# Spreading W_down's sums over the gate/up pairs, placing GpSimd's part beside PSUM reads, moving two pairs' weight prefetches into pass 0's last down product, and putting four additions first there

## The chip, the cores and the metric

The kernel runs on one core of a Trainium2 chip. The metric is the time of one execution in microseconds (us), measured on the device. Engines are named as in the profile: PE is TensorE's matmul, PEld its weight load, DVE VectorE, ACT ScalarE, POOL GpSimd, SP SyncE; "SPq" marks SyncE's queue, which here only issues DMAs. TensorE writes its results into banks of PSUM; to evacuate a bank is to read the result out, after which TensorE may use the bank again. SBUF holds everything else.

## The reference

A pre-norm linear-attention block with a residual, then a pre-norm gated MLP with a residual, all in bf16. The sequence has 2048 tokens, the model width is D = 1024, and the MLP is F = 3584 wide. The change touches the MLP only:

```python
def _B_ref(x, W_gate, W_up, W_down):
    gate = jnp.einsum("bsd,df->bsf", x, W_gate)
    up = jnp.einsum("bsd,df->bsf", x, W_up)
    gate = gate * (gate > 0)                       # shortened
    h = gate * up
    return jnp.einsum("bsf,fd->bsd", h, W_down)

h = x + _A_ref(_layernorm(x), A_wqkv, A_wo)        # attention, not touched
h2 = h + _B_ref(_layernorm(h), B_W_gate, B_W_up, B_W_down)
```

## The kernel before

Every large product is done in Strassen's manner: fewer matmuls, paid for with sums of blocks before them and after them. The MLP runs in two passes of 1024 tokens. A pass has a **gate/up stage** of 14 pairs (pair 0 to 13; a pair is two F-tiles of gate and two of up), and then a **down stage** of seven products, numbered 0 to 6. Products 0, 2 and 4 are plain; 1, 3, 5 and 6 are split once more, each into seven smaller products M1 to M7 ("level 2").

The split products need sums of blocks of W_down. They are made once, during pass 0's gate/up stage, written to DRAM (`t_scr`, `l_scr`), and loaded again chunk by chunk in the down stages, through a ring of seven buffers in SBUF (the "W_down ring"). Three kinds of sums are made: four per pair on VectorE (`WT`), four per two pairs on VectorE (`WL`, sums of the first sums), and four per two pairs on GpSimd (`WM`, from the raw weights).

```python
def wd_sums(q):                       # WT: 4 subtractions of 128x512 on VectorE, then a store
    add(0, wb(0, 1), wb(0, 0), ...)
    add(2, wb(1, 1), wb(0, 1), ...)
    add(1, wb(1, 1), wsum[:, k, 0, :], ...)
    add(3, wb(1, 0), wsum[:, k, 1, :], ...)
    dma(sl_ws[k], t_v[:, :, q, :], wsum[:, k, :, :], ...)

def wl_sums(m):                       # WL: half(0), half(1) on VectorE; WM: raw() on GpSimd
    ...
    def addw(j, x, y):
        PL.add("pool", lambda e: e.tensor_tensor(out=lsw[:, z, j, :], in0=x[0], in1=y[0], op=ALU.subtract),
               reads=x[1] + y[1], writes=[B_lsw[z][j]], name="WM%d_%d" % (j, m))
    def raw():
        addw(0, wr(0, 1), wr(0, 0)); addw(2, wr(1, 1), wr(0, 1))
        addw(1, wr(1, 1), t_(0));    addw(3, wr(1, 0), t_(1))
        dma(sl_lw[z], l_v[:, no, :, m, :], lsw[:, z], ...)
    return [lambda: half(0), lambda: half(1), raw]
```

A pair is seven products, each for gate and for up, each of eight matmuls of 512 columns. The work of the other engines is woven in through the lists `mid`. `PL` keeps one list per engine; an engine does its list strictly in order and waits by semaphores for what it reads.

```python
def strassen_pair(ps_, q, fill, mid):
    ...                                # P1 (copies of the banks on ScalarE), P5, P6
    for f_ in mid[0]: f_()             # <- place A: W_down's sums, before the evacuations of P2
    for w in range(2):
        prod(w, BA[w], w_blk(w, 1, 0), a_blk(1, 0), False, "P2")
        ...
    mul(hh[:, f1, 0:SBW], bank(BA[1]), r11[:, rr, :], ...)
    for w in range(2):
        prod(w, BB[w], t_blk(w, 2), s_blk(2), False, "P7")
        add_s5(c22[:, w, :], bank(BB[w]), B_bank[BB[w]], w, B_c22[w], "c22")   # VectorE reads PSUM
    ...
    for w in range(2):
        prod(w, BC_[w], w_blk(w, 1, 1), s_blk(3), False, "P3")
        add_s5(c12[:, w, :], bank(BC_[w]), B_bank[BC_[w]], w, B_c12[w], "c12")
    for f_ in mid[1]: f_()             # <- place B: behind P3's evacuations
    for w in range(2):
        prod(w, BB[w], t_blk(w, 3), a_blk(1, 1), False, "P4")   # its bank is free after c22
    ...
    load_w_next(); load_w_next()       # gate and up weights, two pairs ahead
```

Pair 13 was left free of sums, so that W_down's first chunks could be loaded there; pair 12 made the sums of both:

```python
wt_at = {q: [q] for q in range(NPAIR - 1)}
wt_at[NPAIR - 2].append(NPAIR - 1)           # pair 12 makes the WT sums of 12 and of 13
...
for x in wt_at.get(q, []):
    mid[0] += wl_q; wl_q.clear()
    mid[1 if q == 0 else 0].append(lambda x=x: wd_sums(x))
    if x % 2 == 1:                            # both pairs of an m are there
        w0_, w1_, wr_ = wl_sums(x // 2)
        mid[1].append(w0_); wl_q.append(w1_); mid[0].append(wr_)
        for z in (x + 1, x + 2):
            if z < NPAIR: mid[0].append(lambda z=z: load_wraw(z))   # raw W_down for the next two
if q not in wt_at:                            # pair 13
    mid[0] += wl_q + [load_wd_next] * NWS     # seven W_down loads
```

In the down stage, the results are put together from PSUM and from SBUF, some by VectorE and some by GpSimd:

```python
level2(5, YB, q_hh(1, hh), sg_x0, ev_out(1, 0, STB, B_V, out2, ...))   # needs V, the residual added
level2(6, XB, q_d4, sg_x1, ev_out(0, 1, 0, B_U, outst, ...))
at(3, 4, lambda: ld_h(0, 1))                  # residual loads
at(4, 0, lambda: ld_h(1, 1), *[add_h(U_, B_U, 0, 1, j) ...])
at(4, 2, lambda: ld_h(1, 0))
at(5, 0, *[add_h(V_, B_V, 1, 0, j) ...],      # GpSimd: V += residual, four additions
         *[p_22(j) ...],                      # GpSimd: four outputs
         e_u5(0), e_u5(1))                    # VectorE: U += PSUM ("dU5"), frees a bank
at(5, 1, e_u5(2), e_u5(3))
```

## Time and profile before

| | before |
|---|---|
| median of 3 runs, us | 735.58 (735.56 to 735.62) |
| profiled span, us | 736.1 |
| TensorE busy, us | 725.6 |
| VectorE busy, us | 561.1 |
| gate/up stage, pass 0 / pass 1, us | 170.37 / 169.21 |
| down stage, pass 0, us | 80.74 |
| last down stage to the end, us | 82.99 |

The stage lengths are differences of the start of a stage's first matmul and of the next stage's, read from the timeline.

Two lines of the profile page of before, the span and the busy time of each engine with its number of instructions:

```profile
span 736.1 us, 11563 instructions
...
PE 725.6 (99%) x4311; PEld 364.0 (49%) x4311; DVE 561.1 (76%) x976; ACT 352.3 (48%) x614; POOL 105.5 (14%) x169
```

TensorE is busy 99% of the span, so a change that keeps every matmul can win only TensorE's idle time. The list of TensorE's waits in before (engine, what it made, what it waited for; us in total, times, longest) says how much that is:

```profile
PE ps L710 <- DVE RAB L1423: 1.0, 2, 0.8
PE ps L710 <- DVE RE L1341: 0.9, 1, 0.9
...
PE ps L710 <- DMA RW<-in_B_W_down_dram: 0.5, 1, 0.5
```

The lines left out lie in the attention part. These three sum to 2.4 us in four places; the first has two. (A wait is counted from the modelled end of the matmul before it, which the records put 0.38 us after its start for 512 columns, while the starts lie 0.22 us apart. So a listed wait costs TensorE about 0.16 us more than it says, as an estimate from these records.) The place of the 0.9 us is pair 12 of pass 0. From the timeline of before there (start, length, engine, line, what it made from what, count, and in brackets the idle time before it):

```profile
377.89 1.89 PE L710 MATMUL ps<-RH,RWG 128*128 128x512 bf16 x8
...
379.49 0.77 DVE L1304 TENSOR_TENSOR RAB<-RAB 128x512 f16<-128x512 bf16 x1
...
380.90 1.04 DVE L1289 TENSOR_TENSOR RO<-RWG,RO 128x1024 f16<-128x1024 bf16 x1
381.35 2.19 POOL L694 TENSOR_TENSOR RAB<-RW,RAB 128x256 f16<-128x256 bf16 x2
381.86 1.15 DVE L1289 TENSOR_TENSOR RO<-RWG 128x1024 f16<-128x1024 bf16 x1
382.94 1.61 DVE L677 TENSOR_TENSOR RX<-RW,RX 128x768 f16<-128x768 f16 x2
384.47 3.01 DVE L655 TENSOR_TENSOR RW<-RW 128x512 f16<-128x512 bf16 x8
387.40 0.69 DVE L1345 TENSOR_TENSOR RAB<-ps,RAB 128x512 bf16<-128x512 f32 x1
388.60 1.88 DVE L1341 TENSOR_TENSOR RE<-ps,RE 128x512 bf16<-128x512 f32 x3
389.34 1.90 PE L710 MATMUL ps<-RH,RO 128*128 128x512 bf16 x8 [0.93 <-DVE RE L1341]
```

The pair starts at 377.89. VectorE makes all eight `WT` sums (L655, 384.47 to 387.40) before it reads P2's and P7's results out of PSUM (L1345, L1341); P4, at 389.34, needs a bank that the first L1341 frees, and waits 0.93 us. VectorE's sums of the next pair's weights (L1289) take 1.04 and 1.15 us beside GpSimd's sums (POOL L694), and 0.68 us elsewhere.

The other waits lie in the last two down products. From the timeline of before there:

```profile
464.79 4.50 POOL L1423 TENSOR_TENSOR RE<-RE,RX 128x512 f32<-128x512 f32 x4 [5.13 <-DVE RE L1423]
...
467.09 2.61 DVE L1423 TENSOR_TENSOR RE<-ps,RE 128x512 f32<-128x512 f32 x4 [1.77 <-POOL RE L1423]
...
469.62 2.00 DVE L1423 TENSOR_TENSOR RAB<-ps,RE 128x512 bf16<-128x512 f32 x3
470.95 1.70 PE L710 MATMUL ps<-RW,RAB 128*128 128x256 f16 x14 [0.80 <-DVE RAB L1423]
...
473.19 1.05 PE L710 MATMUL ps<-RW,RAB 128*128 128x256 bf16 x8 [0.53 <-DMA RW<-in_B_W_down_dram]
```

GpSimd adds the residual to V in four additions, 464.79 to 469.29. VectorE's four sums at 467.09 are two that read V and then two of dU5. TensorE waits 0.80 us for an output's bank and, one product later, 0.53 us for a load of W_down.

### The profile page before, as it was taken

To read this page: it belongs to the slowest core of one execution; us is meant where nothing else is said; L and a number is where in the kernel's file an instruction comes from. 1 tells how busy PE (TensorE), PEld (TensorE's weight loads), DVE (VectorE), ACT (ScalarE), POOL (GpSimd) and SP (SyncE) were. 2 spreads that over 40 slices of the span, in tenths; PEclk is the share of its full clock that TensorE was granted. 3 is DMA by queue.
4 is the path that set the end of the run, shared out by engine and by line. 5 is a ranking of instruction groups with operands and counts; after the bars stand their busy time and mean duration, and the time that the engine had idled before them with its cause. 6 is when DMAs were issued, how large, how long until landed. Compare 5 with 4: busy or idle time off the path is not lost.

```text
span 736.1 us, 11563 instructions
## 1 busy us (share of the span) xinstructions
PE 725.6 (99%) x4311; PEld 364.0 (49%) x4311; DVE 561.1 (76%) x976; ACT 352.3 (48%) x614; POOL 105.5 (14%) x169
## 2 busy tenths in 40 slices
PE   8999999999999999999999999999999999999998
PEld 3444444344444444444444666754444444447766
DVE  6887867799776999898997769865757575667594
ACT  3877756864842456777754100135454544521000
POOL 1311100000360112132220003400000000000052
PEclk9999999999999999999999999999999999999999
DMA  9633144013998889888969999983323242337892
GB/s 304 210 79 94 29 116 163 22 29 67 200 233 254 246 253 274 240 241 256 307 193 301 324 247 341 308 260 85 100 72 106 65 115 59 100 91 245 241 317 87
DMA packets 191880, 133.93 MB, mean 182 GB/s; under 512 B 51664, under 2 KB 173776, under 8 KB 191824
## 3 DMA queue, kind: packets, MB, share of 16 engines
q1 hardware_dynamic: 191152, 132.54, 63.3%
q8 instruction: 34, 0.56, 0.3%
q10 hardware_dynamic: 672, 0.66, 0.3%
q14 instruction: 22, 0.18, 0.1%
HBM read 96.47 MB, written 25.17 MB: 165 GB/s over the span
## 4 chain that ended last, share of the span: by engine, by line
PE 85%; DVE 8%; ACT 2%; DMA 2%; SPq 1%; issue 1%; POOL 0%; DVEq 0%; POOLq 0%; ACTq 0%
PE ps L710 84%; DVE RAB L1423 2%; DMA RW<-in_B_W_down_dram 1%; DVE RAB L796 1%; SPq L545 1%; ACT RX L789 1%; DVE RE L1171 1%; DMA RE<-in_A_x_dram 1%; DVE RX L793 1%; SPq L541 1%; DVE RO L1289 0%; ACT ps L715 0%; ACT RXH L748 0%; DVE RX L1012 0%; DVE RE L1423 0%
## 5 line engine op out<-in xcount | busy, mean ns | idle before, releaser
L715 ACT ACTIVATE ps<-ps 128x512 f32<-128x512 f32 x172 | 100.2, 582 | 212.6 <-PE ps L710 170.3
L710 PE MATMUL ps<-RC,RO 128*128 128x512 f16 x672 | 154.2, 379 | 0.0
L710 PE MATMUL ps<-RH,RWG 128*128 128x512 bf16 x448 | 105.9, 379 | 0.0
L710 PEld LDWEIGHTS ps<-RC,RO 128*128 128x128 f16 x672 | 65.7, 98 | 79.3
L1345 DVE TENSOR_TENSOR RAB<-ps,RAB 128x512 bf16<-128x512 f32 x56 | 38.6, 689 | 71.9 <-PE ps L710 71.9
L710 PE MATMUL ps<-RC,RWG 128*128 128x512 f16 x320 | 76.8, 380 | 0.1
L1341 DVE TENSOR_TENSOR RE<-ps,RE 128x512 bf16<-128x512 f32 x112 | 74.2, 685 | 1.6 <-PE ps L710 0.7
L710 PEld LDWEIGHTS ps<-RH,RWG 128*128 128x128 bf16 x448 | 43.8, 98 | 52.7
L710 PE MATMUL ps<-RW,RAB 128*128 128x256 f16 (+3 forms) x414 | 66.9, 318 | 1.3 <-DVE RAB L1423 0.8
L1423 POOL TENSOR_TENSOR RE<-RE,RX 128x512 f32<-128x512 f32 x16 | 23.6, 1505 | 307.1 <-DMA RX<-h_scr 298.5
L715 ACT ACTIVATE RE<-RE 128x512 bf16<-128x512 bf16 x56 | 35.1, 627 | 64.2 <-DVE RE L1341 63.6
L710 PE MATMUL ps<-RH,RO 128*128 128x512 bf16 (+1 forms) x256 | 61.3, 380 | 0.9 <-DVE RE L1341 0.9
L710 PE MATMUL ps<-RAB 128*128 128x512 bf16 (+2 forms) x274 | 59.3, 357 | 0.1
L710 PE MATMUL ps<-RW,RE 128*128 128x512 bf16 x256 | 57.6, 380 | 0.8 <-DVE RXH L1195 0.7
L715 ACT ACTIVATE RE<-ps 128x512 f32<-128x512 f32 x64 | 37.6, 597 | 35.4 <-PE ps L710 35.0
L710 PEld LDWEIGHTS ps<-RW,RAB 128*128 128x128 bf16 (+1 forms) x414 | 40.3, 98 | 25.8 <-DVE RAB L1423 1.1
L710 PEld LDWEIGHTS ps<-RC,RWG 128*128 128x128 bf16 (+1 forms) x320 | 30.0, 98 | 39.9 <-ACT ps L715 5.9
L1289 DVE TENSOR_TENSOR RO<-RWG 128x1024 f16<-128x1024 bf16 x54 | 39.7, 736 | 4.7 <-DMA RWG<-in_B_W_up_dram 4.7
L1423 DVE TENSOR_TENSOR RE<-ps,RE 128x512 f32<-128x512 f32 x40 | 27.0, 687 | 19.0 <-PE ps L710 15.8
L715 ACT ACTIVATE RAB<-ps 128x512 bf16<-128x512 f32 x56 | 33.4, 596 | 15.0 <-PE ps L710 13.9
L710 PEld LDWEIGHTS ps<-RH,RO 128*128 128x128 f16 (+1 forms) x256 | 24.2, 98 | 31.4 <-DVE RE L1341 1.8
L710 PEld LDWEIGHTS ps<-RAB 128*128 128x128 bf16 (+1 forms) x274 | 26.8, 99 | 25.4 <-issue 1.6
(138 smaller groups left out, 998.0 us busy)
## 6 DMA issues: line engine op xcount, KB each, us to landing
RWG<-in_B_W_gate_dram SPq DMA_DIRECT2D x28, 512.0 KB, 4.8
RWG<-in_B_W_up_dram SPq DMA_DIRECT2D x28, 512.0 KB, 5.9
RW<-in_B_W_down_dram SPq DMA_DIRECT2D x14, 512.0 KB, 6.0
t_scr<-RW SPq DMA_DIRECT2D x14, 512.0 KB, 3.5
RE<-in_A_x_dram SPq DMA_DIRECT2D x23, 256.0 KB, 3.4
RW<-l_scr SPq DMA_DIRECT2D x13, 448.0 KB, 6.3
l_scr<-RX SPq DMA_DIRECT2D x7, 768.0 KB, 4.5
RW<-in_B_W_down_dram SPq DMA_DIRECT2D x12, 384.0 KB, 5.3
```

The costliest lines, as they stand in the source:

```text
L541: return PL.add(eng, lambda e: e.dma_start(dst_ap, src_ap), reads=reads, writes=writes, slot=slot, name=name)
L545: return PL.add("sp", lambda e: e.dma_start_transpose(dst_ap, src_ap), reads=reads, writes=writes, slot=slot, name=name)
L710: lambda e: e.matmul(out_ap, lhsT, rhs, start=start, stop=stop, skip_group_check=skip),
L715: PL.add("act", lambda e: e.activation(out=dst, in_=src, func=func), reads=reads, writes=writes, name=name)
L789: PL.add("act", lambda e: e.activation(out=Et[:, k, :], in_=src, func=ACTF.Exp), reads=[src_buf], writes=[B_E[k]], name=name + "_exp")
L793: PL.add("dve", lambda e: e.tensor_scalar(out=Et[:, k, :], in0=Et[:, k, :], scalar1=1.0, scalar2=1e-6, op0=ALU.min, op1=ALU.add), reads=[] ...
L796: PL.add("dve", lambda e: e.scalar_tensor_tensor(out=dst_ap, in0=src, scalar=C1, in1=Et[:, k, :], op0=ALU.add, op1=ALU.max), reads=[src_bu ...
L1171: PL.add("dve", lambda e: e.tensor_tensor(out=osb[:, k, :].rearrange("p (g h e) -> p g h e", h=HPG, e=Dh), in0=nv[:, :, :, 0:Dh], in1=rden ...
L1289: PL.add(eng, lambda e: e.tensor_tensor(out=tb(j, u), in0=f0(u), in1=f1(u), op=ALU.subtract), reads=[B_w[i + x] for x in r] + ([B_T[k + x] ...
L1341: PL.add("dve", lambda e: e.tensor_tensor(out=dst, in0=src, in1=ftmp[:, w, :], op=ALU.add), reads=[bsrc, B_s5[w]], writes=[bdst], name=name)
L1345: PL.add("dve", lambda e: e.tensor_tensor(out=dst, in0=a_, in1=b_, op=ALU.mult), reads=reads, writes=[wr], name=name)
L1423: PL.add(eng, lambda e: e.tensor_tensor(out=dst, in0=in0, in1=in1, op=op), reads=reads, writes=writes, name=name)
```

## The change

The intent is to take the pile of sums out of pair 12, and to keep GpSimd from slowing VectorE. It has four parts.

- **Spread.** Each pair makes the `WT` sums of one pair; pair 13 makes its own, and the last `WL` sums. In even pairs the `WT` sums stand behind P3 (place B) rather than ahead of P2 (place A). W_down's first loads are spread over pair 13 for that, and the ring's order is rotated, since four of its buffers lie over those of the sums.
- **GpSimd.** The `WM` sums go one by one, each started when a product ends (P7 gate, P7 up, P3 gate, P3 up). VectorE then reads PSUM. The raw W_down loads are issued behind the last of the four.
- **Prefetch.** The gate and up weights of pass 1's first pairs (four loads of 512 KB) are loaded in pass 0's last down product rather than in pairs 12 and 13.
- **dU5.** All four dU5 additions stand in front of the additions that read V.

```diff
-        RING = [list(range(NWS))]
+        RING = [[NWS - 2, NWS - 1] + list(range(NWS - 2))]
 ...                                    # wl_sums
-                       reads=x[1] + y[1], ..., name="WM%d_%d" % (j, m))
+                       deps=[PL.prog["pe"][-1]], reads=x[1] + y[1], ..., name="WM%d_%d" % (j, m))
-            def raw(): ...             # four addw and the store
+            def last():
                 addw(3, wr(1, 0), t_(1))
+                if m == NM - 1:
+                    load_wd_next()
+                    load_wd_next()
                 dma(sl_lw[z], l_v[:, no, :, m, :], lsw[:, z], ...)
+                for q in (2 * m + NWR, 2 * m + NWR + 1):
+                    if q < NPAIR:
+                        load_wraw(q)
+            raw = [lambda: addw(0, ...), lambda: addw(2, ...), lambda: addw(1, ...), last]
 ...                                    # strassen_pair
                 prod(w, BB[w], t_blk(w, 2), s_blk(2), False, "P7")
+                run(mid[4], 1)
 ...
                 prod(w, BC_[w], w_blk(w, 1, 1), s_blk(3), False, "P3")
+                run(mid[4], 1)
 ...
-            load_w_next()
-            load_w_next()
+            if ps_ > 0 or q < NPAIR - 2:
+                load_w_next()
+                load_w_next()
 ...                                    # down_pass
-               lambda: e_u5(0), lambda: e_u5(1))
-            at(5, 1, lambda: e_u5(2), lambda: e_u5(3))
+               *[lambda j=j: e_u5(j) for j in range(STB)])
 ...                                    # the loop over pairs
-        wt_at = {q: [q] for q in range(NPAIR - 1)}
-        wt_at[NPAIR - 2].append(NPAIR - 1)
 ...
+                    mid[0] += wl_q
+                    wl_q.clear()
+                    if q % 2 == 0:
+                        mid[1].append(lambda: wd_sums(q))
+                    else:
+                        w0_, w1_, mid[4] = wl_sums(q // 2)
+                        mid[0].append(lambda: wd_sums(q))
+                        if q < NPAIR - 1:
+                            mid[1].append(w0_)
+                            wl_q.append(w1_)
+                        else:
+                            mid[0] = [load_wd_next] * 2 + mid[0] + [w0_, w1_]
                 strassen_pair(p_, q, fill, mid)
+                if p_ == 0 and q == NPAIR - 1:
+                    for _ in range(NWS - 4):
+                        load_wd_next()
 ...                                    # what down_pass of pass 0 also does
+                late += [(load_w_next, (6, 0))] * 2 + [(load_w_next, (6, 3))] * 2
```

More of the change, by code (lines that the diff above doesn't have):

```diff
@@ L476, in bass_sequential_preLN__linear_attn_block__glu_gated_reglu__prompt_kernel @@
             b_.over = B_wraw + flat(B_wsum)
+        for b_ in B_wd[0:2]:
+            b_.over = list(B_wraw)
         for b_ in flat(B_lsw):
@@ L601, in bass_sequential_preLN__linear_attn_block__glu_gated_reglu__prompt_kernel @@
         X_AT = [(NPAIR - 3) * 2 + i for i in range(NWX)]
-        RING = [list(range(NWS))]
-        RING.append([(len(WLIST) + i) % NWS for i in range(NWS)] +
+        RING = [[NWS - 2, NWS - 1] + list(range(NWS - 2))]
+        RING.append([RING[0][(len(WLIST) + i) % NWS] for i in range(NWS)] +
                     [NWS + (NPAIR * 2 + x) % NWG for x in X_AT])
@@ L694, in addw, with t_ @@
                 PL.add("pool", lambda e: e.tensor_tensor(out=lsw[:, z, j, :], in0=x[0], in1=y[0], op=ALU.subtract),
-                       reads=x[1] + y[1], writes=[B_lsw[z][j]], name="WM%d_%d" % (j, m))
-            def raw():
-                def t_(j):
-                    return lsw[:, z, j, :], [B_lsw[z][j]]
-                addw(0, wr(0, 1), wr(0, 0))
-                addw(2, wr(1, 1), wr(0, 1))
-                addw(1, wr(1, 1), t_(0))
+                       deps=[PL.prog["pe"][-1]], reads=x[1] + y[1], writes=[B_lsw[z][j]], name="WM%d_%d" % (j, m))
+            def t_(j):
+                return lsw[:, z, j, :], [B_lsw[z][j]]
+            def last():
                 addw(3, wr(1, 0), t_(1))
+                if m == NM - 1:
+                    load_wd_next()
+                    load_wd_next()
                 dma(sl_lw[z], l_v[:, no, :, m, :], lsw[:, z], "st_wm_%d" % m, reads=B_lsw[z], writes=[B_wscr[m]])
+                for q in (2 * m + NWR, 2 * m + NWR + 1):
+                    if q < NPAIR:
+                        load_wraw(q)
+            raw = [lambda: addw(0, wr(0, 1), wr(0, 0)), lambda: addw(2, wr(1, 1), wr(0, 1)),
+                   lambda: addw(1, wr(1, 1), t_(0)), last]
             return [lambda: half(0), lambda: half(1), raw]
@@ L1905, in bass_sequential_preLN__linear_attn_block__glu_gated_reglu__prompt_kernel @@
                     hh_sums(q - 1)
-                mid = [[], [], [], []]
+                mid = [[], [], [], [], []]
                 if p_ == 0:
@@ L1916, in bass_sequential_preLN__linear_attn_block__glu_gated_reglu__prompt_kernel @@
                         ln_q.append(n_)
-                    for x in wt_at.get(q, []):
-                        mid[0] += wl_q
-                        wl_q.clear()
-                        mid[1 if q == 0 else 0].append(lambda x=x: wd_sums(x))
-                        if x % 2 == 1:
-                            w0_, w1_, wr_ = wl_sums(x // 2)
+                    mid[0] += wl_q
[6 more added lines that the diff above has]
+                        if q < NPAIR - 1:
                             mid[1].append(w0_)
                             wl_q.append(w1_)
-                            mid[0].append(wr_)
-                            for z in (x + 1, x + 2):
-                                if z < NPAIR:
-                                    mid[0].append(lambda z=z: load_wraw(z))
-                    if q not in wt_at:
-                        mid[0] += wl_q + [load_wd_next] * NWS
-                        wl_q.clear()
+                        else:
+                            mid[0] = [load_wd_next] * 2 + mid[0] + [w0_, w1_]
                 strassen_pair(p_, q, fill, mid)
+                if p_ == 0 and q == NPAIR - 1:
+                    for _ in range(NWS - 4):
+                        load_wd_next()
                 if p_ == 1 and q >= NPAIR - 3:
```

## The prediction

> **What bounds it now.** TensorE. The page's busy table gives 725.6 of 736.1 us; the chain of waits is 85% TensorE. In the gate/up stage (220 to 380 us) the table of windows shows 94 to 95 matmuls per 20 us; the timeline has eight 512-column matmuls in 1.73 us, 216 ns each, the warm rate of the Trainium skill ("TensorE: Matmul & The Clock Gate", "Wait — 56ns, not 53.3ns?": 215.7 ns). The change alters no matmul, only ring slots. It can win only idle TensorE time, and the list of waits has little:
> - 0.93 us at 389.3 (last-but-one pair, pass 0), released by VectorE: W_down's last two F-tile pairs are summed together there, eight 0.4 us subtractions ahead of the evacuations;
> - 0.80 us at 470.9, released by VectorE, and 0.53 us at 473.2, released by a W_down load (last down products of pass 0);
> - 0.18 us at 720.3, VectorE, the same place in pass 1.
>
> Sum 2.4 us (0.33%). The rest is untouched.
>
> **Pair 12, pass 0.** Four sums and two level-2 sums (2.7 us of VectorE) go to pair 13, which makes no sums for a next pair. The 0.93 us gap should vanish.
>
> **Last down products.** All four dU5 additions now stand before the additions that wait 1.77 us for GpSimd (at 467.1). Two of them (1.3 us) fill that idle time, so the bank is free 1.3 us earlier: the 0.80 and 0.18 us gaps go. But the next product's W_down load lands at 473.14, behind a chain of SyncE issues (454.2 to 465.0, one transpose issue of 5.1 us in it) and an 8.1 us transfer with the DMA engines full (share above 1). The change moves none of these, so the 0.80 us mostly reappears as a longer wait for this load (0.53 to about 1.3 us): 0.2 us won.
>
> **Moved prefetches.** Two pairs of gate and up loads (2 MB, about 7 us at 290 GB/s) leave 389 to 406 for the last product (475 to 487). Issued near 480, they should land near 487; VectorE wants them near 485, TensorE at 497. VectorE loses 1 to 2 us, TensorE nothing. W_down's third chunk loads only after GpSimd's last sum, some 11.3 us into pair 13, and is needed at 17.2; such a load took 5.7 us. Tight.
>
> **GpSimd.** Its 28 sums (0.67 us at best, up to 1.19) now each start after a product ends, beside VectorE's PSUM reads. The Trainium skill ("SBUF — State Buffer", "SBUF: two separate sides") says that GpSimd and a VectorE instruction with two SBUF inputs exclude each other; the trace agrees: VectorE sums of 0.68 us took up to 1.15 us. VectorE regains a few us, worth nothing.
>
> **Sum.** 735.6 − 0.93 − 0.18 − 0.2 = 734.3 us. Range 733.1 to 735.5. Chances: faster by over 2% 0.005, within 2% 0.99, slower 0.005.
>
> **Right or wrong shown by:** no wait over 0.2 us between 380 and 400; near 470 no VectorE release and a W_down release of 1 to 1.5 us; no TensorE wait in the first down product (402 to 415) or at pass 1's start (483 to 500); GpSimd's sums nearer 0.67 us; TensorE busy unchanged at 725.6.
>
> **Wrong if:** the last product's load lands earlier (733.2 or so); the late third W_down chunk or late gate/up weights stall TensorE by 1 to 3 us (736 to 738); VectorE's moved sums delay evacuations in the even pairs, seven times over.

## The result, and the profile after

| | before | after |
|---|---|---|
| median of 6 runs, us | 735.6 (734.93 to 736.43) | 734.4 (733.69 to 735.02) |
| ratio, with 95% interval | | 0.9983 (0.9970 to 0.9996) |
| gate/up stage, pass 0, us | 170.37 | 169.21 |
| down stage, pass 0, us | 80.74 | 79.87 |
| last down stage to the end, us | 82.99 | 83.67 |
| VectorE busy, us | 561.1 | 554.0 |

A ratio is the mean time of one kernel's fast runs over the mean of the other's of the same rounds, so it is not quite the ratio of the medians. The change wins about 1.2 us. The profiled spans differ by 3.0 us, and that must not be read as the gain. The profiled execution of before took 737.83 us, more than any run in the table, and 1.65 us of the difference lies at the start: the gate/up stage of pass 0 begins at 232.79 us in before and at 231.14 us in after, long before anything that was changed; between 10 and 20 us the granted TensorE clock was 0.85 in that trace and 1.00 in after's.

The same lines of the page of after:

```profile
span 733.1 us, 11513 instructions
...
PE 719.6 (98%) x4253; PEld 363.4 (50%) x4311; DVE 554.0 (76%) x976; ACT 352.7 (48%) x614; POOL 104.5 (14%) x169
```

TensorE's busy time seems to have shrunk by 6 us. It has not: 58 of the 4311 matmul records are missing from this trace (x4253), while the weight loads are all there. So busy times of TensorE are not compared; the starts of matmuls and the listed waits are. One of the missing records is pass 1's first matmul: the trace's first is at 480.44, but its weight load starts at 480.11, and in before, where both are recorded, the matmul starts 0.11 us after that load. So the down stage is taken to end at 480.22, in all traces with this gap 0.22 us before the first matmul recorded. The weight loads alone give the same gain for the stage, 0.86 us. TensorE's waits in after:

```profile
PE ps L718 <- DVE RAB L1434: 1.5, 2, 0.9
```

The list has more lines, all of them outside the MLP. L1434 is L1423 of before; the line numbers moved. Both waits are in down stages: 0.64 us in pass 0 and 0.87 us in pass 1. The wait in pair 12 and the one for W_down are gone. Pair 12 in after, at the same two products:

```profile
384.56 2.00 DVE L1349 TENSOR_TENSOR RE<-ps,RE 128x512 bf16<-128x512 f32 x3
...
386.75 1.67 PE L718 MATMUL ps<-RH,RO 128*128 128x512 bf16 x7
...
387.42 1.54 DVE L657 TENSOR_TENSOR RW<-RW 128x512 f16<-128x512 bf16 x4
```

VectorE has evacuated P7 and P3 before it makes sums, and the sums are four; they stand behind P3. P4 (386.75; one of eight records is missing) does not wait. GpSimd's sums now lie in pair 13, where this is the last of the four:

```profile
398.93 0.67 POOL L696 TENSOR_TENSOR RAB<-RW,RAB 128x256 f16<-128x256 bf16 x1 [0.19 <-PE ps L718]
398.94 0.68 DVE L1349 TENSOR_TENSOR RE<-ps,RE 128x512 bf16<-128x512 f32 x1
399.67 0.90 SPq L543 DMA_DIRECT2D RW<-in_B_W_down_dram  x2
400.35 1.89 PE L718 MATMUL ps<-RE,RAB 128*128 128x512 bf16 x8
```

The four of pair 13 take 0.67 us each, here beside VectorE's evacuation of PSUM, which takes its usual 0.68 us. In the six odd pairs before it the first of four still takes 0.92 us, so that the mean of all 28 falls only from 0.79 to 0.75 us. VectorE's mean for the sums that GpSimd used to slow fell from 736 to 684 ns. The third W_down chunk is issued at 399.67, as soon as GpSimd's last sum allows it. The down stage starts at 400.35 and never waits for that chunk.

The last two down products in after:

```profile
462.10 4.50 POOL L1434 TENSOR_TENSOR RE<-RE,RX 128x512 f32<-128x512 f32 x4 [5.26 <-DMA RX<-h_scr]
...
464.41 1.42 DVE L1434 TENSOR_TENSOR RE<-ps,RE 128x512 f32<-128x512 f32 x2 [0.71 <-POOL RE L1434]
...
466.64 2.01 DVE L1434 TENSOR_TENSOR RAB<-ps,RE 128x512 bf16<-128x512 f32 x3 [0.81 <-POOL RE L1434]
467.98 3.23 PE L718 MATMUL ps<-RE,RAB 128*128 128x256 f16 x28 [0.64 <-DVE RAB L1434]
```

The dU5 additions are out of the way. Yet VectorE's outputs start at 466.64, just as GpSimd's fourth addition ends (462.10 + 4.50 = 466.60), and TensorE waits for them as it did. In before they started at 469.62, 0.33 us after that end (469.29): this is all that the dU5 additions had held up. Counted from the start of the down stage (403.16 in before, 400.35 in after), TensorE goes on after this wait at 67.79 us in before and at 67.63 us in after. That is a gain of 0.16 us, though the residual's load landed 0.12 us later in the stage. The rest of the stage's gain of 0.87 us is the load's wait, which is not there.

The moved prefetches show on VectorE only. From the timeline of after, at pass 1's start (480.22):

```profile
484.55 0.69 DVE L1297 TENSOR_TENSOR RO<-RWG 128x1024 f16<-128x1024 bf16 x1 [3.43 <-DMA RWG<-in_B_W_up_dram]
```

VectorE waits 3.43 us for the up weights of the next pair. No wait of TensorE follows.

### The profile page after: what moved, and what is told of

It reads as the page before. It is cut to its first block, busy times and chain, and to the rows that moved or that the text cites. A ratio compares the mean times of both kernels' runs of the same rounds, so it can differ in the third digit from the quotient of the medians.

```text
span 733.1 us, 11513 instructions
## 1 busy us (share of the span) xinstructions
PE 719.6 (98%) x4253; PEld 363.4 (50%) x4311; DVE 554.0 (76%) x976; ACT 352.7 (48%) x614; POOL 104.5 (14%) x169
## 4 chain that ended last, share of the span: by engine, by line
PE 86%; DVE 5%; ACT 3%; issue 2%; DMA 2%; SPq 1%; POOL 0%; POOLq 0%; ACTq 0%; DVEq 0%
PE ps L718 86%; SPq L543 1%; DVE RAB L804 1%; DMA RE<-in_A_x_dram 1%; DVE RE L1179 1%; ACT RX L797 1%; ACT RXH L756 1%; DMA RE<-RE 1%; DVE RX L801 1%; DVE RX L1020 1%; POOL RE L1434 0%; DMA RX<-h_scr 0%; ACT ps L723 0%; DVE RW L914 0%; DVE RXH L1203 0%
## 5 line engine op out<-in xcount | busy, mean ns | idle before, releaser
L1434 POOL TENSOR_TENSOR RE<-RE,RX 128x512 f32<-128x512 f32 x16 | 23.5, 1494 | 288.2 <-DMA RX<-h_scr 288.2
L718 PE MATMUL ps<-RW,RAB 128*128 128x256 f16 (+3 forms) x399 | 62.5, 312 | 0.3
L718 PE MATMUL ps<-RH,RO 128*128 128x512 bf16 (+1 forms) x228 | 55.3, 379 | 1.5
L718 PE MATMUL ps<-RAB 128*128 128x512 bf16 (+1 forms) x254 | 53.7, 350 | 0.3
L718 PEld LDWEIGHTS ps<-RW,RAB 128*128 128x128 f16 (+1 forms) x404 | 39.6, 98 | 21.2
L1297 DVE TENSOR_TENSOR RO<-RWG 128x1024 f16<-128x1024 bf16 x54 | 36.9, 684 | 8.3 <-DMA RWG<-in_B_W_up_dram 8.3
L1434 DVE TENSOR_TENSOR RE<-ps,RE 128x512 f32<-128x512 f32 x40 | 27.0, 688 | 18.1 <-PE ps L718 15.4
L718 PEld LDWEIGHTS ps<-RW,RE 128*128 128x128 bf16 x256 | 23.9, 98 | 29.1 <-DVE RXH L1203 1.2
```

The lines of the kernel that those rows point to most:

```text
L718: lambda e: e.matmul(out_ap, lhsT, rhs, start=start, stop=stop, skip_group_check=skip),
L1297: PL.add(eng, lambda e: e.tensor_tensor(out=tb(j, u), in0=f0(u), in1=f1(u), op=ALU.subtract), reads=[B_w[i + x] for x in r] + ([B_T[k + x] ...
L1434: PL.add(eng, lambda e: e.tensor_tensor(out=dst, in0=in0, in1=in1, op=op), reads=reads, writes=writes, name=name)
```

## The experiments

Twelve runs were made, ten of edited kernels and one each of before and after again. Times are compared by their ratios. All gave correct results. The times first, each with its ratio against before in the same rounds. Then the two stages of pass 0 in the profiled run, and all of TensorE's waits there from 0.17 us on.

| kernel | median, us | ratio (95%) | gate/up | down | waits in pass 0: gate/up; down |
|---|---|---|---|---|---|
| before (first trace) | 735.6 | | 170.37 | 80.74 | 0.93 VectorE; 0.80 VectorE, 0.53 load |
| before_again | 736.4 | 1.0007 (0.9989 to 1.0024) | 171.73 | 80.53 | 0.96 VectorE and three small; 0.80 load, 0.27 VectorE |
| after | 734.4 | 0.9983 (0.9970 to 0.9996) | 169.21 | 79.87 | none; 0.64 VectorE |
| control | 733.77 | 0.9975 (0.9963 to 0.9988) | 169.22 | 79.96 | none; 0.74 VectorE |
| undo_eu5 | 733.97 | 0.9982 (0.9969 to 0.9994) | 169.22 | 80.54 | none; 0.47 load, 0.55 VectorE |
| undo_spread | 733.29 | 0.9974 (0.9961 to 0.9986) | 169.21 | 80.60 | none; 1.39 load |
| undo_prefetch | 734.74 | 0.9988 (0.9974 to 1.0002) | 169.24 | 80.92 | none; 0.45 load, 0.65 VectorE |
| only_pool | 736.6 | 1.0014 (1.0000 to 1.0029) | 171.96 | 80.74 | 1.28 and three smaller, VectorE; 0.57 load, 0.52 VectorE |
| undo_pool | 734.36 | 0.9982 (0.9969 to 0.9995) | 169.22 | 80.23 | none; 0.80 VectorE |
| undo_both | 735.09 | 0.9992 (0.9979 to 1.0004) | 170.46 | 80.82 | 1.08 VectorE; 1.37 VectorE |
| pool_place | 734.35 | 0.9988 (0.9974 to 1.0002) | 169.21 | 80.88 | none; 0.94 load, 0.54 VectorE |
| ht_early | 732.79 | 0.9971 (0.9958 to 0.9983) | 169.21 | 79.25 | none; none |
| split_adds | 736.12 | 1.0015 (1.0002 to 1.0028) | 169.21 | 80.56 | none; 1.33 VectorE |
| split_only | 735.83 | 1.0017 (1.0004 to 1.0030) | 169.21 | 80.94 | none; 1.71 VectorE |

In the nine traces in which the record of pass 1's first matmul is missing, the down stage is taken to end 0.22 us before the first one recorded, as in after. The stage that nothing disturbs, pass 1's gate/up, then took 169.2 us in all fourteen traces (169.11 us in each by the weight loads, which are all there). So stages compare far more finely than the times of whole runs do.

### control

The changed kernel as it is.

> The changed kernel again, unedited, to see which differences of the two traces come back. Between the two traces on hand the stages differ so: pair 12 of pass 0 takes 12.1 us against 13.2, the down stage of pass 0 79.9 against 80.7, the last down stage to the end 83.7 against 83.0, everything before pair 12 differs by 1.7 us (clock warm-up and start, not the change). Theory S (the differences are systematic): the same lengths within 0.2 us, the VectorE wait of 0.9 us near the end of pass 1's down stage again, time 734.4, ratio to before 0.998. Rival N (pass 1's 0.9 us wait and the early W_down load are chance): the wait in pass 1 is back near 0.2 us, or the W_down wait near 470 us is back.

733.77 us (732.89 to 733.98), ratio 0.9975: the gain is there again. The 0.74 us wait for VectorE in the last down products is there again too, and no wait for W_down. Pass 1 shows no wait at all in its down stage, where after's trace had 0.87 us. The same code therefore gives 0 and 0.87 us at that place, and nothing there is put down to the change.

### undo_eu5

The dU5 part taken back.

```diff
-               *[lambda j=j: e_u5(j) for j in range(STB)])
+               lambda: e_u5(0), lambda: e_u5(1))
+            at(5, 1, lambda: e_u5(2), lambda: e_u5(3))
```

> The changed kernel with the four dU5 additions at their old places (two after the second down sub-product). As predicted blind: VectorE is 1.3 us later at the bank, so the wait near 468 us grows from 0.64 to about 1.9 us less slack, and the time by 0.5 to 1.3 us in pass 0 and as much in pass 1. Rival (after reading the trace: the two outputs wait for GpSimd's fourth addition, which waits for the residual load, and the dU5 additions stand in idle time either way): the wait grows by at most 0.3 us in each pass, time at most 0.6 us longer.

The wait for VectorE is 0.55 us, not longer than the 0.64 and 0.74 us of the changed kernel, but a load's wait of 0.47 us ahead of it hides part of it. The time, 733.97 us, is within noise of control's. What the time can't resolve, the timeline of undo_eu5 shows:

```profile
461.89 4.50 POOL L1434 TENSOR_TENSOR RE<-RE,RX 128x512 f32<-128x512 f32 x4 [4.40 <-DMA RX<-h_scr]
...
466.71 2.00 DVE L1434 TENSOR_TENSOR RAB<-ps,RE 128x512 bf16<-128x512 f32 x3
```

GpSimd ends at 466.39, and the outputs start 0.33 us later, as in before. So it is in all five traces with the old place of the dU5 additions; in the seven with the new place and four additions on GpSimd, the outputs start 0.03 us after GpSimd's end. The dU5 part is worth 0.30 us in front of the outputs, of the 1.3 us that the prediction gave it; the rest was idle time either way.

### undo_spread

The pile put back: pair 12 makes the `WT` sums of both pairs ahead of P2, with the `WL` halves placed as before. GpSimd's sums stay one by one in pair 13.

```diff
-                    if q % 2 == 0:
+                    if q == NPAIR - 2:
+                        w0_, w1_, wm_ = wl_sums(q // 2)
+                        mid[0] += [lambda: wd_sums(q), lambda: wd_sums(q + 1)]
+                        mid[1].append(w0_)
+                    elif q == NPAIR - 1:
+                        mid[4] = wm_
+                        mid[0] += [load_wd_next] * 2 + [w1_]
+                    elif q % 2 == 0:
```

> The changed kernel with the sums of W_down's last F-tile pair moved back into pair 12, beside that pair's own. Theory: the 0.9 to 1.1 us TensorE wait for VectorE in pair 12 comes back whole, pair 12 is 13.1 to 13.2 us long, time up by 0.9 to 1.1 us against the control. Rival (the new places of the other sums, or GpSimd keeping off VectorE's sums, removed the wait): pair 12 stays below 12.4 us.

If the pile alone made the wait, it had to come back. It did not: pair 12 has no wait and the stage takes 169.21 us. The timeline of undo_spread in pair 12:

```profile
375.90 1.89 PE L718 MATMUL ps<-RH,RWG 128*128 128x512 bf16 x8
...
377.75 0.43 DVE L1312 TENSOR_TENSOR RAB<-RAB 128x512 f16<-128x512 bf16 x1
...
379.43 0.68 DVE L1297 TENSOR_TENSOR RO<-RWG 128x1024 f16<-128x1024 bf16 x1
380.03 1.14 DVE L679 TENSOR_TENSOR RX<-RW,RX 128x768 f16<-128x768 f16 x2
381.09 3.02 DVE L657 TENSOR_TENSOR RW<-RW 128x512 f16<-128x512 bf16 x8
384.02 0.68 DVE L1353 TENSOR_TENSOR RAB<-ps,RAB 128x512 bf16<-128x512 f32 x1
...
386.47 1.67 PE L718 MATMUL ps<-RH,RO 128*128 128x512 bf16 x7
```

VectorE has the same list as in before, eight sums at a stretch included. From the pair's start to the evacuation behind them it takes 384.02 − 375.90 = 8.1 us; in before it took 387.40 − 377.89 = 9.5 us. The eight sums last 3.0 us in both. The difference is in the instructions ahead of them, which GpSimd's sums stretched in before: 0.77 us against 0.43 for one sum of the hidden activations, 1.04 and 1.15 against 0.69 and 0.68 for two of the next pair's weights, 1.61 against 1.14 for the two `WL` sums. That is 1.6 us, of which 1.4 us reach the evacuation. P4 (386.47) does not wait. The theory that the pile alone is the cause falls; the rival, GpSimd beside a crowded VectorE, holds so far.

The down stage of this run has a wait of 1.39 us for a load of the stored sums. It is taken up under pool_place.

### undo_prefetch

The four gate and up loads put back into pairs 12 and 13.

```diff
-            if ps_ > 0 or q < NPAIR - 2:
-                load_w_next()
-                load_w_next()
+            load_w_next()
+            load_w_next()
...
-                late += [(load_w_next, (6, 0))] * 2 + [(load_w_next, (6, 3))] * 2
```

> The changed kernel with the four gate and up loads back at the ends of pairs 12 and 13. Theory P (the 2 MB taken out of the queue let the last product's W_down load arrive 1 us earlier): a W_down wait of 0.5 us or more comes back near 470 us, and the down stage of pass 0 is 80.4 us or longer. Rival (as predicted blind, the queue is the same from 430 us on, and the load's landing varies by itself): no W_down wait over 0.2 us, the down stage within 0.2 us of the control. In both the first VectorE sums of pass 1 no longer wait 3.4 us for gate/up weights, and TensorE gains nothing from that.

The down stage takes 80.92 us (control 79.96); the time is 734.74 us, 1.0 us over control's. The two intervals against before overlap (0.9974 to 1.0002 and 0.9963 to 0.9988), but the two kernels ran in the same rounds, and each of this kernel's five runs (734.01 and up) took longer than each of control's (733.98 and less). So the moved prefetches very likely win something. How is less clear. Theory P expected a W_down wait near 470 us, and none came. Instead this one trace has a wait of 0.45 us for a stored sum at 422.5, which the other traces do not have at that place. It fits that the moved prefetches make room for W_down's loads, which the changed kernel issues later than before did; this is not shown.

### before_again

The kernel before, profiled a second time, to see which of its waits repeat.

> The kernel before, unedited: a second trace of it. What is systematic comes back: pair 12 about 1.1 us longer than 12.1 (gate/up stage of pass 0 about 170.3 us from the first pair to the first down matmul, where every version with GpSimd moved had 169.2). What is chance does not: the W_down wait of 0.53 us near 473 us and the 0.18 us near the end. Theory D (the waits before the last down product are set by when single loads land, and vary by half a microsecond from run to run): the down stage of pass 0 again has 1 to 2 us of waits, but split otherwise between VectorE and a load. Rival: 0.80 VectorE and 0.53 W_down again within 0.1 us.

Pair 12 has a wait of 0.96 us for VectorE: it repeats. The last down products have waits of 0.80 us and 0.27 us, a sum of 1.07 where the first trace has 1.33, but now the longer one is for a load (of `l_scr`) and the shorter for VectorE. Which of the two releases TensorE is not fixed. The gate/up stage was longer than in the first trace, 171.73 us; three small waits that the first trace did not have (0.38, 0.22, 0.27 us, near 242 to 267 us) are 0.87 of the 1.36 us.

### only_pool

The GpSimd part alone, on the kernel before: sums one by one beside PSUM reads, raw loads behind the last.

```diff
-                       reads=x[1] + y[1], writes=[B_lsw[z][j]], name="WM%d_%d" % (j, m))
+                       deps=[PL.prog["pe"][-1]], reads=x[1] + y[1], writes=[B_lsw[z][j]], name="WM%d_%d" % (j, m))
-            def raw(): ...
+            def last(): ...       # as in the change, without its W_down loads
+                for q in (2 * m + NWR, 2 * m + NWR + 1):
+                    if q < NPAIR:
+                        load_wraw(q)
...
+                run(mid[4], 1)    # behind P7 and behind P3, as in the change
...
-                            mid[0].append(wr_)
-                            for z in (x + 1, x + 2):
-                                if z < NPAIR:
-                                    mid[0].append(lambda z=z: load_wraw(z))
+                            mid[4] = wr_
```

> The kernel before with GpSimd's part of the change alone: its four sums of each two pairs one by one behind a product each, the raw loads after the last; all of VectorE's sums stay where they were, so both last pairs are still summed in pair 12. Theory G (it was GpSimd's sums beside VectorE's that made VectorE late in pair 12: in the trace they stretch its instructions there by 1.6 us, and without them the same list of VectorE instructions ended in time): no TensorE wait in pair 12, gate/up stage of pass 0 169.2 us, time about 1 us below the kernel before. Rival (as predicted blind, GpSimd's deference is worth nothing by itself): the wait of 0.9 us stays and the time is that of the kernel before.

The wait in pair 12 is gone, as undo_spread led one to think. But the kernel is not faster than before: 736.6 us. Even pairs now have waits, one of 1.28 us and three of 0.18 to 0.34. The timeline at the longest:

```profile
305.59 1.21 SPq L541 DMA_DIRECT2D RW<-in_B_W_down_dram  x2
...
311.45 1.56 DVE L655 TENSOR_TENSOR RW<-RW 128x512 f16<-128x512 bf16 x4 [3.02 <-DMA RW<-in_B_W_down_dram]
...
314.86 1.90 PE L713 MATMUL ps<-RH,RO 128*128 128x512 bf16 x8 [1.28 <-DVE RE L1344]
```

The raw weights are loaded only when GpSimd has read the last of them, which is late in the odd pair or, as here, 2 us into the next one (it starts at 303.06; GpSimd's last two sums take 303.57 to 305.14). The next pair's `WT` sums stand ahead of P2 and wait 3.02 us for the load, and all evacuations wait behind them. VectorE's list of waits has this line four times, 9.0 us in all. So the GpSimd part needs the other move, the sums of even pairs behind P3, or it costs more than it wins.

### undo_pool

The changed kernel with GpSimd's sums put together again, without their wait for a product; the spread stays.

```diff
-                       deps=[PL.prog["pe"][-1]], reads=x[1] + y[1], writes=[B_lsw[z][j]], name="WM%d_%d" % (j, m))
+                       reads=x[1] + y[1], writes=[B_lsw[z][j]], name="WM%d_%d" % (j, m))
...
+                        mid[0] += mid[4]
+                        mid[4] = []
```

> The changed kernel with GpSimd's sums back in one go in the middle of each odd pair, without their wait for a product. VectorE's sums stay spread. If spreading alone is enough too: no TensorE wait in the gate/up stage, 169.2 us, though GpSimd's sums stretch VectorE's instructions again (VectorE busy 5 us or more above the control's). If GpSimd's deference is what is needed everywhere: a wait of 0.3 us or more in some odd pair. Time within 0.5 us of the control in the first case.

No wait in pairs 12 and 13, gate/up 169.22 us, 734.36 us in all. The contention was there: GpSimd's last four sums ran in pair 12 again (377.97 to 382.23), beside VectorE instructions that took 1.04 us for 0.69 and 1.96 for 1.14, and VectorE was busy 4.6 us longer over the span than in control. Without the pile, it cost TensorE nothing. So each of the two measures takes the wait away alone.

### undo_both

Both taken back: the pile in pair 12, and GpSimd's sums together beside it. Prefetches, ring and dU5 stay as changed.

```diff
-                       deps=[PL.prog["pe"][-1]], reads=..., name="WM%d_%d" % (j, m))
+                       reads=..., name="WM%d_%d" % (j, m))
...
+                    if q == NPAIR - 2:
+                        w0_, w1_, wm_ = wl_sums(q // 2)
+                        mid[0] += [lambda: wd_sums(q), lambda: wd_sums(q + 1)] + wm_
+                        mid[1].append(w0_)
+                    elif q == NPAIR - 1:
+                        mid[0] += [load_wd_next] * 2 + [w1_]
```

> The changed kernel with both undone for pair 12: both last pairs' sums in pair 12 and GpSimd's sums beside them, without their wait. Theory (either of the two measures is enough; the wait needs both, pile-up and GpSimd): the wait of 0.5 to 1 us in pair 12 is back, gate/up stage 169.7 to 170.4 us. Rival (something else in the change removed it): 169.2 us.

The wait is back. The timeline of undo_both in pair 12, which starts at 375.25:

```profile
378.55 1.16 DVE L1297 TENSOR_TENSOR RO<-RWG 128x1024 f16<-128x1024 bf16 x1
...
380.20 1.92 POOL L696 TENSOR_TENSOR RAB<-RW,RAB 128x256 f16<-128x256 bf16 x2
...
381.51 3.48 DVE L657 TENSOR_TENSOR RW<-RW 128x512 f16<-128x512 bf16 x8
...
386.85 1.90 PE L718 MATMUL ps<-RH,RO 128*128 128x512 bf16 x8 [1.08 <-DVE RE L1349]
```

The instructions are stretched once more (1.16 us for 0.68, 3.48 for 3.02), the wait is 1.08 us, and the stage takes 170.46 us, 1.2 us more than with either measure. With undo_spread and undo_pool this closes the square: the wait needs the pile and the contention together.

### pool_place

On the kernel before: the GpSimd part of only_pool, and the `WT` sums of the even pairs up to 10 behind P3. Pair 12 keeps its pile, the ring, the prefetches and dU5 stay as before.

```diff
 (only_pool's edit, and)
-                        mid[1 if q == 0 else 0].append(lambda x=x: wd_sums(x))
+                        mid[1 if q % 2 == 0 and q < NPAIR - 2 else 0].append(lambda x=x: wd_sums(x))
```

> The GpSimd-alone kernel with one more piece of the change: in the even pairs before pair 12 the four W_down sums stand behind the P3 product, as in the changed kernel. Both last pairs are still summed in pair 12. In the GpSimd-alone kernel VectorE waited 9.0 us in four even pairs for W_down's raw loads (they now start only after GpSimd's last sum), and TensorE then 0.2 to 1.3 us for VectorE. Theory R (the later raw loads are the whole cost of GpSimd's deference, and the later place of the sums pays it off): no VectorE wait for raw loads, no TensorE wait in the gate/up stage, 169.2 us, time 1 to 2.5 us below the GpSimd-alone kernel. Rival: waits of 0.2 us or more stay in the even pairs.

VectorE's waits for raw weights are gone from its list, and gate/up takes 169.21 us: the whole gain of the stage, with the pile still in place. The time is 734.35 us (ratio 0.9988), against 736.6 us for only_pool (1.0014). Its down stage has a load's wait of 0.94 us.

That load's wait can be set beside the other traces. The four traces with the old order of the W_down ring (before, before_again, only_pool, pool_place) all have a wait of 0.53 to 0.94 us for a load in the last two down products. Of the ten traces with the new order only two have one there (undo_eu5 0.47, undo_spread 1.39). The load that is late is another one from trace to trace: W_down itself, `l_scr` or `t_scr`. So the order of the loads probably matters, but no run changed the ring alone, and this is not shown.

### ht_early

An attempt at a better version, on the changed kernel: one of the residual loads four units earlier, and two of the transposed loads of the next pass moved from product 4 to product 1, so that what GpSimd's additions wait for comes sooner through SyncE's list.

```diff
-            at(3, 4, lambda: ld_h(0, 1))
+            at(3, 0, lambda: ld_h(0, 1))
...
-                slots_ = [(0, 1), (0, 3), (2, 0), (2, 1), (2, 2), (2, 3), (4, 1), (4, 2)]
+                slots_ = [(0, 1), (0, 3), (1, 2), (1, 4), (2, 0), (2, 1), (2, 2), (2, 3)]
```

> The changed kernel with the residual loads for the third set of outputs issued right after the first level-2 product of the fourth down sub-stage rather than four products later, and the two transposes that hold SyncE 4.7 and 1.3 us just before the fourth set of residual loads moved to the second sub-stage. Theory H (the wait before the last product is residual load, then GpSimd's additions, then VectorE's outputs, then TensorE; SyncE's transposes and the late first loads put it behind): GpSimd's additions end 1.5 us or more earlier against TensorE, no VectorE wait of TensorE near 467 and near 717 us, down stage of pass 0 79.4 to 79.6 us, time 0.7 to 1.4 us below the changed kernel's. Rival (the DMA queue is full from 435 to 490 us whatever the order, so the wait only moves to a W_down load or to an earlier product): 0.5 us or more of waits stay in the down stage of pass 0 and the time is the changed kernel's within 0.4 us.

The timeline of ht_early in the last two down products:

```profile
461.02 4.51 POOL L1434 TENSOR_TENSOR RE<-RE,RX 128x512 f32<-128x512 f32 x4 [6.77 <-DMA RX<-h_scr]
...
465.56 2.12 DVE L1434 TENSOR_TENSOR RAB<-ps,RE 128x512 bf16<-128x512 f32 x3 [0.81 <-POOL RE L1434]
466.91 3.23 PE L718 MATMUL ps<-RE,RAB 128*128 128x256 f16 x28
```

GpSimd's additions ended about 0.6 us earlier in the stage than in after, not the 1.5 us that were hoped for. It is just enough: TensorE has no wait at all in pass 0's down stage, which takes 79.25 us, the shortest of all traces. The chain from the residual's load over GpSimd to VectorE's outputs is what the wait of 0.64 to 0.80 us hangs on. The other traces agree: in all fourteen, before included, GpSimd's additions start 0.13 to 0.14 us after the third residual load has landed. The time is 732.79 us, ratio 0.9971: the best, clearly below before, but not separable from control (0.9975) by these runs. Pass 1 keeps its wait in this run (0.77 us).

### split_adds

The other way to shorten that chain, on top of ht_early: two of the four additions to V on VectorE, so that GpSimd has two.

```diff
-            order = (2, 3, 0, 1)
+            order = (2, 3)
...
-               *[lambda j=j: e_u5(j) for j in range(STB)])
+               *[lambda j=j: e_u5(j) for j in range(STB)],
+               *[lambda j=j: add_h(V_, B_V, 1, 0, j, "dve") for j in range(2)])
```

> The kernel of the run before (earlier residual loads, two transposes moved) with two of the four residual additions ahead of the last sub-product's outputs on VectorE instead of GpSimd. In the traces four additions of 1.13 us on GpSimd (4.5 us) stand between VectorE's four d22 additions and its outputs, and TensorE needs the outputs some 9 us after the fourth sub-stage ends: no slack, so any late residual load becomes a TensorE wait of 0.2 to 0.9 us, in pass 1 above all (0, 0.18 to 0.87 us in ten traces). Theory C (that chain sets these waits): VectorE's outputs come 1.5 us or more earlier, no TensorE wait over 0.2 us for VectorE near the end of either pass, time 732.0 to 732.6, 0.2 to 0.8 below the run before. Rival (the loads themselves are what is late, whoever adds): the wait in pass 1 stays at 0.3 us or more.

The kernel got slower, and the wait longer: 1.33 us in pass 0 and 1.10 us in pass 1. The timeline of split_adds:

```profile
460.83 2.27 POOL L1434 TENSOR_TENSOR RE<-RE,RX 128x512 f32<-128x512 f32 x2 [7.00 <-DMA RX<-h_scr]
462.74 2.48 DVE L1434 TENSOR_TENSOR RE<-RE,RX 128x512 f32<-128x512 f32 x2
463.06 5.40 POOL L1434 TENSOR_TENSOR RX<-RO,RX 128x512 bf16<-128x512 f32 x4
...
466.46 2.00 DVE L1434 TENSOR_TENSOR RAB<-ps,RE 128x512 bf16<-128x512 f32 x3
467.79 2.47 PE L718 MATMUL ps<-RE,RAB 128*128 128x256 f16 x21 [1.33 <-DVE RAB L1434]
```

GpSimd ends its two additions at 463.10 and goes on at once to its next work, the four outputs, beside VectorE's two additions with two SBUF inputs each. GpSimd takes 5.40 us for four that took 4.5 us otherwise; VectorE takes 2.48 us for its two (2.86 us in split_only), for which no run has an undisturbed time. VectorE's own list now comes last: behind the two additions stand two sums of V and PSUM that last until 466.54, 3.4 us after GpSimd's end, and the outputs start at 466.46. Counted from the stage's start (399.47, and 399.89 in ht_early) that is 66.99 us, against 65.67 us in ht_early. The expectation failed: VectorE had 0.81 us to spare in front of its outputs, and was given 2.48 us of work.

### split_only

The same split, on the changed kernel, without ht_early's loads; the edit is split_adds' alone.

> The changed kernel with only the two residual additions moved from GpSimd to VectorE; loads and transposes where the change has them. Theory C: the 0.64 to 0.74 us wait near 467 us in pass 0 and the chance wait near the end of pass 1 go, time 733.0 to 733.6. Rival (in pass 0 the residual loads, held up 4.7 us by a transpose on SyncE, are late for either engine, or a W_down load is next in line): a wait of 0.3 us or more for VectorE or a load stays in pass 0.

1.71 us of waiting for VectorE in pass 0, 1.04 us in pass 1, and 735.83 us. The split is to blame, not its combination with the earlier loads. By the ratios to before, split_adds is 3.2 us slower than ht_early and split_only 2.5 us slower than after, while the listed waits of their traces grow by 1.7 and 1.2 us; their profiled runs were the fastest of their runs (734.88 and 735.14 us). What the other runs lost is open.

## Why the prediction was right or wrong

The time was right: 734.3 us predicted, 734.4 us measured, inside the range of 733.1 to 735.5 and within 2% as expected. The sum behind it was right only in its first term, so that the total is in part luck: pass 0's down stage won 0.87 us where 0.2 us was predicted, and in after's trace a longer wait of pass 1 took 0.7 us of it back.

- **TensorE bounds the kernel, and the change can win only waits.** Right. The matmul rate did not change: in the gate/up stages of both kernels eight 512-column matmuls start 1.73 us before the next eight, 216 ns each, where the Trainium skill ("TensorE: Matmul & The Clock Gate", section "Wait — 56ns, not 53.3ns?") has 215.7 ns for a warm array.
- **Pair 12, 0.93 us.** Right in size: the wait went in every trace of the changed kernel, and the stage went from 170.37 to 169.21 us (1.16 us, close to the listed wait plus the 0.16 us that the list leaves out). Incomplete in its cause. Spreading alone does take the gap away, as undo_pool shows. But the prediction put the gap down to the eight subtractions ahead of the evacuations alone; undo_spread keeps those eight and has no gap.
- **GpSimd, "VectorE regains a few us, worth nothing".** This step failed. Its first half held for VectorE: busy time down by 7 us, the mean of the disturbed sums 736 to 684 ns. GpSimd's own sums came to 0.67 us in pair 13, but to 0.75 us in the mean of all 28 (before 0.79). But in pair 12 the contention was worth the whole gap of 0.93 us: there, VectorE's list was so full that 1.6 us of stretching came out as a wait of TensorE. Undo_both against undo_spread shows it, 1.08 us against none, 170.46 against 169.21 us. Because undo_pool too has no gap, the two parts of the change are worth one gap together, not one each.
- **Last down products, "0.2 us won".** This step failed in both halves. The 0.80 us wait for VectorE was to go and to reappear as a longer wait for a W_down load. In fact the wait for VectorE stayed, 0.64 us (control 0.74), and the load's wait of 0.53 us went. First half, "the bank is free 1.3 us earlier": the prediction had seen that VectorE waits 1.77 us for GpSimd before the sums that read V, and filled that idle time with dU5. It overlooked that the outputs wait for GpSimd's last addition too, at 466.60 in after; filling the time ahead of that won the 0.30 us by which VectorE's list had run past it, and no more. Undo_eu5 (outputs 0.33 us after GpSimd's end) and ht_early (GpSimd earlier, no wait) show it from both sides. Second half, "the change moves none of these": the prediction took the landing of the W_down load in one trace as fixed. Counted from the stage's start it landed at 69.98 us in before, at 69.41 us in before_again, which is the same kernel, and at 68.90 us in after, issued within half a microsecond of the same moment each time. Whether anything in the change made it land earlier, or chance did, stays open. The stage won 0.87 us in after's trace and 0.78 us in control's, where 0.2 was predicted.
- **Pass 1, 0.18 us.** Not confirmed. Traces of one and the same kernel have 0.18 and 0.37 us (before), and 0.87 and 0 us (the changed kernel). This term is chance.
- **Moved prefetches: VectorE loses 1 to 2 us, TensorE nothing.** Right for TensorE; VectorE's wait was mis-sized, 3.43 us. The prediction counted no gain for them, and undo_prefetch makes it very likely that they win something, about 1 us by its times and its trace.
- **The tight third W_down chunk.** Right: issued 0.7 us before the down stage starts, and nothing waited for it.
- **The risk of even pairs, named under "wrong if".** It did not come true in the change as it is, since the sums stand behind P3 there. Only_pool shows that the danger was real, one step beside where the prediction looked: with the sums ahead of P2, the later raw loads delay the evacuations.

By the traces, the change wins 1.2 us in pair 12 (170.37 to 169.21) and about 0.8 us in pass 0's down stage, 2.0 us in sum; the measured medians differ by 1.2 us in the first comparison and by 1.6 us for control (735.35 to 733.77). Pass 1's last wait, which comes and goes by up to 0.9 us, is of the size of what lies between them.

## What to carry to other kernels

A wait can need two causes at once, here a full list on VectorE and GpSimd slowing that list; take each away alone before you say which it was, since either may be enough. Before you fill an engine's idle time, look at everything that the work behind the gap waits for: if it also waits for the end of the same other engine's work, filling the gap wins only what your list ran past that end (here 0.30 us of 1.3). And where parts of a change move buffers' last readers later, as GpSimd's sums did with the raw loads, try each part alone: a part that helps in company may cost by itself.

## What the Trainium skill lacked or had wrong

- "SBUF — State Buffer", section "SBUF: two separate sides", says that a GpSimd instruction and a VectorE instruction with two SBUF inputs exclude each other for the whole instruction, and that VectorE's own pair of ports never waits. The traces agree: VectorE's sums of 0.68 us took up to 1.15 us, and the evacuations that read PSUM kept their 0.68 us beside GpSimd's sums of 0.67 us. What the page lacks is how this looks in a profile: not as a wait with a releaser, but as a longer instruction. No list of waits shows it; one finds it only by comparing the mean of a group (736 ns against 684 ns) or single instructions.
- "GPSIMD Engine Reference", section "8. Key points", has VectorE about twice as fast for elementwise work. Here GpSimd took 0.67 us for a 16-bit sum of 128x256 and VectorE 0.38 us for one of 128x512 (3.01 us for eight), about 3.5 times per element. For sums of f32 over 128x512 it was 1.13 us (4.50 us for four) against 0.69 us with one input in PSUM, 1.6 times.
- No page has a figure in time for how long one transposing DMA holds SyncE's queue, behind which all later loads of this kernel stand ("DMA: Bandwidth & Descriptors", where it would belong, has only cycles of the sequencer, without the transfer, in a comparison with trn3). In the trace of before the eight transposing loads of one form in the down stage took 1.23 to 5.11 us each to issue; what makes one four times as long as another is open.
